# A written order on TensorE for the routing rounds of a two-layer mixture of experts: 27 steps of three held-back products in each round

## The chip, the core and the metric

The kernel runs on one core of a Trainium2 chip. The metric is the time of one execution on the device in microseconds, as the median of several runs. Five engines work in parallel, each through its own queue of instructions in order: TensorE (PE) multiplies matrices into PSUM banks, VectorE (DVE) and ScalarE (ACT) work elementwise, GpSimd (POOL) does elementwise work, reductions over partitions and indirect DMAs, and SyncE (SP) issues most of the other DMAs. The loading of a matrix into PE ahead of a product is listed apart, as PEld.

## What is computed

Sparse attention, then two mixtures of experts on its output. In the first every token goes through all eight experts, weighted by a Sinkhorn-normalised table; in the second every token gets one expert, taken greedily in the order of the logits, with room for 192 tokens per expert.

```python
x = attention(q, k, v)              # 2 x 8 heads x 768 x 64 -> 1536 tokens x 512
# first layer: N=1536, D=512, E=8 experts, F=1024
P = sinkhorn(exp(x @ w_gate))       # 8 rounds
for e in range(E):
    out += P[:, e:e+1] * (np.maximum(x @ w1[e], 0.0) @ w2[e])
# second layer, on out
logits = x @ w_gate
for idx in np.argsort(-logits.flatten()):
    tok, e = idx // E, idx % E
    if assigned[tok] >= 0 or counts[e] >= cap:   # cap = N // E = 192
        continue
    assigned[tok] = e; counts[e] += 1
for e in range(E):
    mask = assigned == e
    out[mask] = np.maximum(x[mask] @ w1[e], 0.0) @ w2[e]
```

## The kernel before

*Tiles.* Tokens are worked on in 12 blocks of 128 (`NC`), in three token blocks of 512 (`NTB`). Every fp32 operand is split into two fp16 parts, so each contraction over 128 takes three products: high by high, high by low, low by high (`mm3`, lines 664 to 666). A hidden block (`ph`) of one expert and one token block goes into a `hslot`; from it come four accumulations (`py`), one per 128 tokens, of 8 x 3 = 24 products of 512 columns each. The result goes, weighted, into the sum `acc`.

*Held-back work.* The first layer's second products of expert 7 and expert 6 are not done when their hidden blocks are ready. The list `post` holds them: (6,2), (7,0), (7,1), (7,2), (6,0), (6,1), as (expert, token block), in all 6 x 4 x 24 = 576 products. The hidden blocks of (6,0) and (6,1) wait in DRAM and come back (`get_back`) into the slots of the first two entries of `post`, when these are used up. The results of all but the last entry are evicted by ACT (line 760, into one of three `relu` buffers) and added by POOL (line 761); those of the last are added by DVE (line 765). ACT then takes the largest absolute value of each finished block of `acc` (`absj`, line 686). Calls of `expert_out` for `post` are written behind the whole routing.

*Gate.* The logits `L` of the second layer depend linearly on what each expert adds, so the share of expert 7 is worked out ahead of its held-back products: twelve small products `pg` (lines 138 and 139 hold their last two parts), one per 128 tokens, each read from its PSUM bank by two DVE instructions (lines 144 and 145) before the next may use that bank.

*Routing.* Seven rounds (line 918). Each has a `propose` on DVE (each token's best free expert, its weight `w`, the 0/1 table `B8`); 12 transposes `pw` on PE (line 925), which lay the weights out along the free axis, copied out by ACT and DVE (`raw`); comparisons of every weight with every other, by DVE (lines 953, 955, 956) and for token blocks 0, 4 and 8 by ACT (lines 946 to 950), into `xt`; three groups of 12 count products `pr` (line 961), each behind four token blocks of comparisons; copies of the counts (`spill`, lines 971 and 973); 12 products `prc` (line 976); two DVE instructions (lines 978 and 983; X in `rBT`, sum `rT`), for which POOL has prepared `rBT` (lines 932 to 934); one sum over partitions `prs` on PE (line 985); and six DVE instructions that update `L`. Behind the seventh come a last `propose`, 12 products `pk` (lines 999 and 1001), and the slots `si`.

*Behind the routing.* POOL scatters the rows of `acc` to their slots in DRAM (`xg`, line 1034, twelve indirect DMAs), and reduces the largest absolute value `xam` over the partitions (line 102), from which the scale of the second layer follows. Rows of two experts are read back, transposed by PE (`px`, line 1087), scaled by ACT (line 1089), and the second layer begins with `ph`. Its weights, split and put away in DRAM before, come by SP's queue into slots that become free, those of the held-back hidden blocks among them.

*What sets the order.* A scheduler places the instructions of each engine: written order gives the priority, and an instruction whose inputs come late lets later ones go ahead. The held-back products are written last, so they fill what it takes to be gaps: 49 between the twelve gate products, 369 in the first six rounds (61 to 63 in each), 53 in the seventh up to its `prs`, 13 from there to `pk`, and 92 behind `pk`.

Of the kernel before, what the change touches and what calls it, by code (L numbers as in the profile page):

```python
# [20 lines left out]
P = 128  # L21
# [19 lines left out]
def tile_sparse_attention_moe_moe(ctx, tc, q, k, v, ng, nl, wg1, w11, w12, wg2, w21, w22, out, taps=None):  # L41
# [10 lines left out]
    TB = 512  # L52
# [697 lines left out]
    def expert_out(e, tb, by_pool=False):  # L750
# [3 lines left out]
        for t in range(CPB):  # L754
# [3 lines left out]
            if by_pool:  # L758
                y = rawp.tile([P, TB], F32, name="relu", bufs=3)
                nc.scalar.activation(y[:, :DM], ps, AF.Copy, scale=pf[:, c:c + 1])  # L760
                nc.gpsimd.tensor_tensor(acc[:, c, :DM], acc[:, c, :DM], y[:, :DM], op=ALU.add)  # L761
            elif e == 0:
                nc.vector.tensor_scalar(acc[:, c, :DM], ps, pf[:, c:c + 1], None, op0=ALU.mult)
            else:
                nc.vector.scalar_tensor_tensor(acc[:, c, :DM], ps, pf[:, c:c + 1], acc[:, c, :DM],
                                               op0=ALU.mult, op1=ALU.add)

# [147 lines left out]

    NQ = NT // 512
    on_act = (0, 4, 8)
    for rnd in range(E - 1):
        w = propose()
        wr = rawp.tile([P, NT], F32, name="raw", bufs=2)  # L920
        for n in range(NQ):
            pt = aux([P, 4, P], name="pw")
            for c in range(4):
                cc = 4 * n + c
                nc.tensor.transpose(pt[:, c, :], w[:, cc:cc + 1].to_broadcast([P, P]), ident)
            if n == 1:
# [10 lines left out]
        for c in range(NC):  # L937
# [20 lines left out]
            if c % 4 == 3:  # L958
                def count(n, cc):
                    j = 32 * (cc % 4)  # L960
                    return nc.tensor.matmul(pr[n][j:j + 32, :], Bp[:, cc, :], gs[cc][:, n * 512:n * 512 + 512],
                                            start=cc < 4, stop=cc >= NC - 4, tile_position=(0, j))
# [12 lines left out]
        for c in range(NC):  # L975
            nc.tensor.matmul(pc[:, c, :], rs[:, c * P:c * P + P], comb, start=True, stop=True)
# [8 lines left out]
        nc.tensor.matmul(T.rearrange("p a e -> p (a e)"), ones, R.rearrange("p a e -> p (a e)"), start=True, stop=True)  # L985
# [9 lines left out]
    propose()  # L995

    pk = misc([P, NC, E], name="pk")
    for n in range(1, NC):
        nc.tensor.matmul(pk[:, n if n > 1 else 0:, :], onesb, Bz[:, 1 if n > 1 else 0:NC + 1 - n, 0:E],
                         start=n == 1, stop=False)  # L1000
    nc.tensor.matmul(pk, before, B8, start=False, stop=True)
# [11 lines left out]
    for n, (e, tb) in enumerate(post):  # L1013
# [165 lines left out]
```

## Time and profile before

| | us |
|---|---|
| median of 3 runs | 1388.05 (1387.29 to 1388.94) |
| the profiled execution, its own time | 1384.17 |
| its span, from first to last instruction | 1382.3 |
| PE busy | 1308.7 |
| DVE busy | 808.3 |
| ACT busy | 591.8 |
| POOL busy | 211.3 |

Times in the rows below count from the start of the span. Idle time in brackets stands ahead of an instruction, with what ended it. The granted clock is TensorE's: 1.00 is 2.4 GHz, 0.50 is 1.2 GHz; over the whole execution it was 0.987 in the mean. A PE row's length is modelled at its end, so consecutive products overlap; how fast they follow one another is read from the starts.

### The profile page before, as it was taken

How to read it: one execution, taken by the hardware profiler on the slowest of the kernel's cores; microseconds unless marked ns; L12 is line 12 of the kernel's file. 1: busy time of each engine (PE TensorE's matmuls, PEld its weight loads, DVE VectorE, ACT ScalarE, POOL GpSimd, SP SyncE). 2: the span in 40 equal slices, each digit the busy share in tenths (PEclk: the TensorE clock that was granted, in tenths of full speed). 3: DMA queues.
4: the chain of work that ended last, by engine and by line, in shares of the span. 5: the costliest groups of instructions: out<-in, count | busy, mean ns of one | idle time of the engine just before them, and what ended most of it. 6: DMA issues, size and time to landing. Idle time of an engine off the chain costs nothing.

```text
span 1382.3 us, 19944 instructions
## 1 busy us (share of the span) xinstructions
PE 1308.7 (95%) x7956; PEld 670.7 (49%) x7956; DVE 808.3 (58%) x1765; ACT 591.8 (43%) x1053; POOL 211.3 (15%) x323
## 2 busy tenths in 40 slices
PE   5899999999999999999899999999999989879998
PEld 3665544444444444444344444445545434337775
DVE  5777686554666466556546655575635898822121
ACT  3667551343243324333522434166553566613332
POOL 5233211010001000000100010000001333430100
PEclk8999999999999999999999999999999999989999
DMA  8352024151545135324424441431001111378640
GB/s 217 82 150 74 1 74 170 61 197 47 173 145 170 61 126 179 122 87 158 149 95 142 143 160 57 169 123 62 2 1 63 62 62 62 122 208 302 273 201 24
DMA packets 88557, 164.93 MB, mean 119 GB/s; under 512 B 50065, under 2 KB 50065, under 8 KB 85905
## 3 DMA queue, kind: packets, MB, share of 16 engines
q1 hardware_dynamic: 77040, 119.62, 26.7%
q0 software_dynamic: 11424, 44.05, 8.3%
q8 instruction: 62, 1.02, 0.3%
q14 instruction: 31, 0.25, 0.1%
HBM read 119.61 MB, written 44.05 MB: 118 GB/s over the span
## 4 chain that ended last, share of the span: by engine, by line
PE 47%; DVE 15%; issue 15%; DMA 13%; ACT 5%; POOL 5%; POOLq 0%; DVEq 0%; ACTq 0%
DMA raw<-in_moe_w_dram 7%; PE ph L664 7%; PE ph L666 7%; PE ph L665 7%; PE py L664 6%; PE py L665 6%; PE py L666 6%; DMA ws<-spill 6%; DVE wam L607 4%; DVE wslot L619 2%; POOL acc L761 2%; PE pe L491 2%; PE pa L510 2%; DVE xt L953 1%; DVE xt L955 1%
## 5 line engine op out<-in xcount | busy, mean ns | idle before, releaser
L664 PE MATMUL py<-wslot,hslot 128*128 128x512 f16 x768 | 291.3, 379 | 9.9 <-ACT relu L658 9.9
L664 PE MATMUL ph<-xt,wslot 128*128 128x512 f16 x768 | 291.4, 379 | 7.4 <-ACT relu L658 3.9
L665 PE MATMUL py<-wslot,hslot 128*128 128x512 f16 x768 | 291.3, 379 | 0.0
L666 PE MATMUL py<-wslot,hslot 128*128 128x512 f16 x768 | 291.3, 379 | 0.0
L666 PE MATMUL ph<-xt,wslot 128*128 128x512 f16 x768 | 291.3, 379 | 0.0
L665 PE MATMUL ph<-xt,wslot 128*128 128x512 f16 x768 | 291.2, 379 | 0.0
L657 ACT ACTIVATE hslot<-ph 128x512 f16<-128x512 f32 x192 | 114.5, 596 | 208.9 <-PE ph L666 208.7
L659 DVE TENSOR_TENSOR hslot<-relu,hslot 128x512 f16<-128x512 f32 x192 | 131.5, 688 | 119.6 <-ACT relu L658 118.6
L607 DVE TENSOR_REDUCE wam<-raw 128x1 f32<-128x1024 f32 (+1 forms) x136 | 152.5, 1149 | 74.6 <-DMA raw<-in_moe_w_dram 74.5
L618 ACT ACTIVATE spill<-raw,s 128x1024 f16<-128x1024 f32 x64 | 72.8, 1146 | 246.4 <-DVE s L114 129.8
L619 DVE SCALAR_TENSOR_TENSOR spill<-raw,s,spill 128x1024 f16<-128x1024 f32 x64 | 81.7, 1284 | 114.4 <-ACT spill L618 113.2
L658 ACT ACTIVATE relu<-ph 128x512 f32<-128x512 f32 (+1 forms) x224 | 130.1, 581 | 0.0
L665 PEld LDWEIGHTS <-hslot 128*128 128x128 f16 x768 | 75.3, 98 | 98.9 <-issue 13.6
L665 PEld LDWEIGHTS <-wslot 128*128 128x128 f16 x768 | 75.1, 98 | 93.8 <-issue 9.5
L664 PEld LDWEIGHTS <-hslot 128*128 128x128 f16 x768 | 75.3, 98 | 88.6 <-issue 2.5
L666 PEld LDWEIGHTS <-hslot 128*128 128x128 f16 x768 | 75.1, 98 | 88.5 <-issue 2.5
L666 PEld LDWEIGHTS <-wslot 128*128 128x128 f16 x768 | 75.1, 98 | 87.4
L664 PEld LDWEIGHTS <-wslot 128*128 128x128 f16 x768 | 75.1, 98 | 87.4 <-issue 2.4
L618 ACT ACTIVATE wslot<-raw,s 128x1024 f16<-128x1024 f32 (+1 forms) x72 | 70.9, 1047 | 72.3 <-PE py L666 48.7
L619 DVE SCALAR_TENSOR_TENSOR wslot<-raw,s,wslot 128x1024 f16<-128x1024 f32 (+1 forms) x72 | 81.2, 1159 | 4.3 <-ACT wslot L618 4.3
L650 POOL DMA_DIRECT2D ws<-spill x64 | 44.2, 692 | 220.8 <-DVE spill L619 220.5
L102 POOL PARTITION_ALL_REDUCE amax<-wam x30 | 10.6, 354 | 413.9 <-DVE wam L608 406.0
(245 smaller groups left out, 1652.6 us busy)
## 6 DMA issues: line engine op xcount, KB each, us to landing
raw<-in_moe_w_dram SPq DMA_DIRECT2D x64, 1024.0 KB, 5.9
ws<-spill POOLq DMA_DIRECT2D x64, 512.0 KB, 6.6
w2slot<-ws SPq DMA_DIRECT2D x16, 2048.0 KB, 10.2
hd<-hslot POOLq DMA_DIRECT2D x2, 2048.0 KB, 7.2
hslot<-hd SPq DMA_DIRECT2D x2, 2048.0 KB
qb<-in_q_dram SPq DMA_DIRECT2D x12, 256.0 KB, 3.4
kb<-in_k_dram SPq DMA_DIRECT2D x12, 256.0 KB, 6.6
vo<-in_v_dram SPq DMA_DIRECT2D x12, 256.0 KB, 3.7
```

What stands on the lines that cost most here:

```text
L491: nc.tensor.transpose(pe[:ck, y, j, :], ex[:, y, j, a * P:a * P + ck], ident)
L510: nc.tensor.matmul(S.pa[64 * j:64 * j + 64, p, :], S.vs[a][:ck, 2 * p + j, :], ets[a][:ck, y, j, :], start=a == 0, stop=a == S.nch - 1, ti ...
L607: nc.vector.tensor_reduce(am[:, y:y + 1], raw, axis=AX.X, op=ALU.max, apply_absolute_value=True)
L618: nc.scalar.activation(hi, raw, AF.Copy, scale=s[:, 0:1])
L619: nc.vector.scalar_tensor_tensor(lo, raw, s[:, 0:1], hi, op0=ALU.mult, op1=ALU.subtract)
L650: nc.gpsimd.dma_start(dr[:, :, a * q4:a * q4 + q4], t)
L657: nc.scalar.activation(hi, ps, AF.Relu, scale=HS)
L658: nc.scalar.activation(r[:, :n], ps, AF.Relu, scale=HS)
L659: nc.vector.tensor_sub(lo, r[:, :n], hi)
L664: nc.tensor.matmul(out_, lhs(0, a), rhs(0, a), start=a == 0, stop=False)
L665: nc.tensor.matmul(out_, lhs(0, a), rhs(1, a), start=False, stop=False)
L666: nc.tensor.matmul(out_, lhs(1, a), rhs(0, a), start=False, stop=a == n - 1)
```

## The change

The held-back products get a place in the program. `expert_out` for `post` is gone; a generator `held_back` issues the same products, and yields after each step of three. `run(n)` issues the next n steps, and stands in the round at six places: seven steps behind the transposes `pw`, four, eight and two behind the three groups of counts, three behind `prc`, three behind `prs`. So a round has 27 steps, 81 products. Two more steps are behind the last `propose`, ahead of `pk`; what is left of the 192 steps, one, is issued behind the slots.

`pin` is a new mark on PE's instructions (`tc.keep_in_program_order`): those that bear it keep the order in which they are written. All products of the rounds, `pk` and the held-back products bear it. The counts no longer bear the rule that set a group behind its first product (`issue_after`). `get_back` is written ahead of the rounds. How the held-back results are evicted and added stays as it was.

```diff
+    pin = tc.keep_in_program_order
+
+    def held_back(e, tb, by_pool):
...
+        for t in range(CPB):
+            c = tb * CPB + t
+            ps = mmbank([P, DM], name="py")
+            for f in range(FC):
+                for n, (y1, y2) in enumerate(((0, 0), (0, 1), (1, 0))):
+                    pin(nc.tensor.matmul(ps, h[:, y1, f, t * P:t * P + P], w[:, y2, f, :],
+                                         start=f == 0 and n == 0, stop=f == FC - 1 and n == 2))
+                if f == FC - 1:
...
+                yield
...
+    for n, (e, tb) in enumerate(post):
+        if (e, tb) in away:
+            m = n - len(post) + len(away)
+            get_back(e, tb, NTB * post[m][0] + post[m][1])
+
+    def all_held():
+        for e, tb in post:
+            yield from held_back(e, tb, (e, tb) != post[-1])
+
+    held = all_held()
+
+    def run(n):
+
+        for _ in range(n):
+            next(held, None)
+
     NQ = NT // 512
     on_act = (0, 4, 8)
     for rnd in range(E - 1):
...
-                nc.tensor.transpose(pt[:, c, :], w[:, cc:cc + 1].to_broadcast([P, P]), ident)
+                pin(nc.tensor.transpose(pt[:, c, :], w[:, cc:cc + 1].to_broadcast([P, P]), ident))
...
+        run(7)
...
-                first = count(0, c)
-                with tc.issue_after(first.ins):
-                    for n in range(NQ):
-                        for cc in range(c - (n == 0), c - 4, -1):
-                            count(n, cc)
+                    pin(nc.tensor.matmul(pr[n][j:j + 32, :], Bp[:, cc, :], gs[cc][:, n * 512:n * 512 + 512],
+                                         start=cc < 4, stop=cc >= NC - 4, tile_position=(0, j)))
+                for n in range(NQ):
+                    for cc in range(c, c - 4, -1):
+                        count(n, cc)
+                run((4, 8, 2)[c // 4])
...
-            nc.tensor.matmul(pc[:, c, :], rs[:, c * P:c * P + P], comb, start=True, stop=True)
+            pin(nc.tensor.matmul(pc[:, c, :], rs[:, c * P:c * P + P], comb, start=True, stop=True))
+        run(3)
...
+        pin(nc.tensor.matmul(T.rearrange("p a e -> p (a e)"), ones, R.rearrange("p a e -> p (a e)"), start=True,
+                             stop=True))
+        run(3)
...
     propose()
+    run(2)
...
+    finish(held)
...
-    for e, tb in post:
-        expert_out(e, tb, (e, tb) != post[-1])
```

The first place is on PE, between the last gate product and the first round's transposes. Before, with held-back products (`py`) there:

```order
L139 MATMUL pg<-vg7hl,hslot 128x16
L666 LDWEIGHTS hslot
L666 MATMUL py<-wslot,hslot 128x512
L664 LDWEIGHTS hslot
L664 MATMUL py<-wslot,hslot 128x512
L665 LDWEIGHTS hslot
L665 MATMUL py<-wslot,hslot 128x512
L666 LDWEIGHTS hslot
L666 MATMUL py<-wslot,hslot 128x512
L664 LDWEIGHTS hslot
L664 MATMUL py<-wslot,hslot 128x512
L925 MATMUL pw<-ident,rw 128x128 x12
```

and now, where the transposes follow at once:

```order
L138 LDWEIGHTS hslot
L138 MATMUL pg<-vg7hl,hslot 128x16
L139 LDWEIGHTS hslot
L139 MATMUL pg<-vg7hl,hslot 128x16
L961 MATMUL pw<-ident,rw 128x128 x12
```

All 49 products that stood between and behind the gate products have moved into the rounds.

The second place is on ACT, in the sixth round, from the last comparisons (into `xt`) to the next round's copies (`raw`). Before:

```order
L946 ACTIVATE xt<-raw,rw 128x1024
L949 ACTIVATE xt<-raw,rw 128x384
L947 ACTIVATE xt<-xt 128x1024
L950 ACTIVATE xt<-xt,ones 128x384
L760 ACTIVATE relu<-py,pf 128x512
L686 ACTIVATE absj,xam<-acc 128x512 x2
L973 ACTIVATE spill<-pr 128x512 x2
L760 ACTIVATE relu<-py,pf 128x512
L686 ACTIVATE absj,xam<-acc 128x512
L929 ACTIVATE raw<-pw 128x512 x2
```

Now:

```order
L986 ACTIVATE xt<-raw,rw 128x384
L686 ACTIVATE absj,xam<-acc 128x512
L987 ACTIVATE xt<-xt,ones 128x384
L686 ACTIVATE absj,xam<-acc 128x512
L781 ACTIVATE relu<-py,pf 128x512
L686 ACTIVATE absj,xam<-acc 128x512
L1009 ACTIVATE spill<-pr 128x512 x2
L781 ACTIVATE relu<-py,pf 128x512
L686 ACTIVATE absj,xam<-acc 128x512
L965 ACTIVATE raw<-pw 128x512 x2
```

Ahead of the two copies of the counts stand three `absj` with one eviction now, where two `absj` and one eviction stood.

The third place is on POOL, from the last round's `rBT` to the scatters of the output at the kernel's end. The two ISA rows are the load of the reduction's code and the reduction over the partitions. Before:

```order
L934 TENSOR_TENSOR rBT<-rBT,tok 128x96
L761 TENSOR_TENSOR acc<-acc,relu 128x512 x3
L1034 DMA xg<-acc,si 1536x513 x12
L102 ISA
L102 ISA amax<-xam 128x1
L1042 DMA out_dram<-spill,idx 1536x512 x12
```

Now:

```order
L971 TENSOR_TENSOR rBT<-rBT,tok 128x96
L1069 DMA xg<-acc,si 1536x513
L102 ISA
L102 ISA amax<-xam 128x1
L1069 DMA xg<-acc,si 1536x513 x11
L1077 DMA out_dram<-spill,idx 1536x512 x12
```

No add of a held-back result is left behind the seventh round's `rBT`, and the load and the reduction stand behind the first scatter, no longer behind the twelfth. SP's queue has the same order as before.

## Rows read from the trace of the kernel before

**Rows 1.** The head of the profile page: the span of the profiled execution, and the busy time, share of the span and instructions of each engine.

```profile
span 1382.3 us, 19944 instructions
...
PE 1308.7 (95%) x7956; PEld 670.7 (49%) x7956; DVE 808.3 (58%) x1765; ACT 591.8 (43%) x1053; POOL 211.3 (15%) x323
```

**Rows 2.** Busy time by stretch, from the span's start: the stretch and its length; PE busy (instructions), PEld, DVE, ACT, POOL likewise; the granted TensorE clock (1.00 is full speed); the DMA share; GB/s. In order of time these are the gate products after the last hidden product up to the first round's `pw`; the first `pw` to the seventh round's `prs`; within it the second round alone, `pw` to `pw`; the end of the seventh round and the 92 held-back products behind it; and from there to the first product of the second layer.

```profile
1047.35:1062.95 15.60, 15.58 (x242) 9.43 (x241) 9.18 (x39) 1.79 (x4) 1.27 (x1) 1.00 0.38 138
...
1062.95:1208.55 145.60, 128.48 (x855) 58.09 (x855) 127.46 (x301) 93.79 (x130) 56.50 (x39) 1.00 0.19 73
...
1084.01:1104.29 20.28, 18.55 (x124) 8.40 (x124) 18.10 (x45) 12.89 (x17) 9.31 (x5) 1.00 0.14 58
...
1208.55:1232.25 23.70, 23.57 (x119) 10.68 (x119) 5.83 (x19) 3.58 (x9) 11.89 (x12) 1.00 0.76 211
...
1232.25:1242.80 10.55, 2.42 (x10) 1.68 (x10) 1.60 (x8) 1.36 (x4) 1.33 (x2) 0.60 0.50 162
```

**Rows 3.** Timeline of PE in the second round: start and length in us, engine, line, operation, output <- inputs, shapes, count, and in brackets the idle time before it and what ended it.

```profile
1084.01 1.52 PE L925 MATMUL pw<-ident,rw 128*128 128x128 f32 x12
...
1085.37 0.38 PE L666 MATMUL py<-wslot,hslot 128*128 128x512 f16 x1
...
1089.47 0.38 PE L664 MATMUL py<-wslot,hslot 128*128 128x512 f16 x1
...
1097.17 0.38 PE L665 MATMUL py<-wslot,hslot 128*128 128x512 f16 x1
...
1098.74 0.83 PE L961 MATMUL pr<-xt,Bz 128*32 128x512 bf16 x12 [1.19 <-DVE xt L953]
...
1100.41 0.34 PE L976 MATMUL prc<-comb,spill 128*128 128x8 f16 x8
...
1102.18 0.37 PE L985 MATMUL prs<-rT,ones 128*128 128x24 f32 x2 [0.33 <-DVE rT L983]
...
1104.29 1.52 PE L925 MATMUL pw<-ident,rw 128*128 128x128 f32 x12
```

**Rows 4.** Waits from the first `pw` to the seventh `prs`: who waited for whom, us in all, times, the longest.

```profile
ACT absj L686 <- POOL acc L761: 10.1, 7, 2.3
...
PE pr L961 <- DVE xt L953: 7.8, 7, 1.2
...
PE prc L976 <- ACT spill L973: 2.8, 3, 1.3
```

**Rows 5.** Timeline of POOL, DVE, PE and ACT: the add of a held-back product in a pause of DVE (first row), and then the sixth round.

```profile
1080.94 1.09 POOL L761 TENSOR_TENSOR acc<-acc,relu 128x512 f32<-128x512 f32 x1 [3.74 <-ACT relu L760]
...
1175.10 7.99 POOL L761 TENSOR_TENSOR acc<-acc,relu 128x512 f32<-128x512 f32 x2 [5.44 <-ACT relu L760]
...
1178.25 0.34 DVE L955 TENSOR_SCALAR xt<-raw,rw 128x256 bf16<-128x256 f32 x1
...
1179.57 1.18 DVE L955 TENSOR_SCALAR xt<-raw,rw 128x128 bf16<-128x128 f32 x1
...
1181.93 0.83 PE L961 MATMUL pr<-xt,Bz 128*32 128x512 bf16 x12 [1.02 <-DVE xt L953]
...
1183.12 0.63 ACT L686 ACTIVATE absj<-acc 128x512 bf16<-128x512 f32 x1 [1.70 <-POOL acc L761]
...
1183.75 1.06 ACT L973 ACTIVATE spill<-pr 128x512 f16<-128x512 f32 x2
```

**Rows 6.** Timeline of PE and DVE for one of the twelve gate products: its first and last product on PE, and DVE's two instructions that read the PSUM bank.

```profile
1058.94 0.17 PE L138 MATMUL pg<-vg7hl,hslot 128*128 128x16 f16 x1
...
1059.32 0.17 PE L139 MATMUL pg<-vg7hl,hslot 128*128 128x16 f16 x1
...
1059.53 0.23 DVE L144 SCALAR_TENSOR_TENSOR gt<-pg,vfc,L 128x8 f32<-128x8 f32 x1 [0.58 <-PE pg L139]
...
1059.79 0.23 DVE L145 SCALAR_TENSOR_TENSOR L<-pg,vfc,gt 128x8 f32<-128x8 f32 x1
```

**Rows 7.** Busy time by stretch in the attention part, columns as in rows 2.

```profile
46.00:49.00 3.00, 1.05 (x4) 0.67 (x4) 2.98 (x9) 1.10 (x4) 0.10 (x1) 1.00 1.05 238
...
50.00:56.00 6.00, 5.55 (x24) 4.13 (x22) 4.85 (x19) 3.07 (x10) 2.42 (x6) 0.50 0.02 4
```

**Rows 8.** Timeline of PE, POOL and DVE from the last round's `prs` to the first product of the second layer.

```profile
1208.55 0.37 PE L985 MATMUL prs<-rT,ones 128*128 128x24 f32 x2 [0.32 <-DVE rT L983]
...
1211.82 0.47 PE L999 MATMUL pk<-Bz,onesb 128*128 128x96 bf16 x11
...
1213.95 1.20 POOL L1034 DMA_INDIRECT xg<-acc,si  x1 [1.19 <-DVE si L1009]
...
1215.45 0.96 POOL L1034 DMA_INDIRECT xg<-acc,si  x1 [0.30 <-issue]
...
1232.25 0.75 DVE L765 SCALAR_TENSOR_TENSOR acc<-py,pf,acc 128x512 f32<-128x512 f32 x1 [4.43 <-PE py L666]
...
1233.28 0.95 POOL L1034 DMA_INDIRECT xg<-acc,si  x1 [4.22 <-DVE acc L765]
...
1239.45 0.90 PE L1087 MATMUL px<-ident,raw 128*128 128x128 f32 x3 [7.24 <-DMA raw<-xg]
...
1240.30 0.38 POOL L102 PARTITION_ALL_REDUCE amax<-xam  x1 [6.07 <-issue]
...
1242.80 0.80 PE L664 MATMUL ph<-xt,w2slot 128*128 128x192 f16 x4 [0.46 <-ACT xt L1089]
```

More of the change, by code (lines that the diff above doesn't have):

```diff
@@ L748, in factors, with expert_out @@
         pfs[e] = pf
-    def expert_out(e, tb, by_pool=False):
+    def expert_out(e, tb):
         h = hs.pop((e, tb))
@@ L757, in expert_out @@
             mm3(ps, lambda z, f: h[:, z, f, t * P:t * P + P], lambda z, f: w[:, z, f, :], FC)
[L758 to L762, printed above, removed]
+            if e == 0:
                 nc.vector.tensor_scalar(acc[:, c, :DM], ps, pf[:, c:c + 1], None, op0=ALU.mult)
@@ L766, in expert_out @@
                                                op0=ALU.mult, op1=ALU.add)
+    pin = tc.keep_in_program_order
+    def held_back(e, tb, by_pool):
+        h = hs.pop((e, tb))
+        w, _ = W[e, 1]
+        pf = pfs[e]
+        for t in range(CPB):
[6 more added lines that the diff above has]
+                if f == FC - 1:
+                    if by_pool:
+                        y = rawp.tile([P, TB], F32, name="relu", bufs=3)
+                        nc.scalar.activation(y[:, :DM], ps, AF.Copy, scale=pf[:, c:c + 1])
+                        nc.gpsimd.tensor_tensor(acc[:, c, :DM], acc[:, c, :DM], y[:, :DM], op=ALU.add)
+                    else:
+                        nc.vector.scalar_tensor_tensor(acc[:, c, :DM], ps, pf[:, c:c + 1], acc[:, c, :DM],
+                                                       op0=ALU.mult, op1=ALU.add)
+                yield
     waiting = []
@@ L984, in tile_sparse_attention_moe_moe @@
         T = misc([P, 3, E], name="prs")
-        nc.tensor.matmul(T.rearrange("p a e -> p (a e)"), ones, R.rearrange("p a e -> p (a e)"), start=True, stop=True)
+        pin(nc.tensor.matmul(T.rearrange("p a e -> p (a e)"), ones, R.rearrange("p a e -> p (a e)"), start=True,
+                             stop=True))
+        run(3)
         tau = rsm.tile([P, E], F32, name="rtau")
@@ L995, in tile_sparse_attention_moe_moe @@
     propose()
+    run(2)
     pk = misc([P, NC, E], name="pk")
     for n in range(1, NC):
-        nc.tensor.matmul(pk[:, n if n > 1 else 0:, :], onesb, Bz[:, 1 if n > 1 else 0:NC + 1 - n, 0:E],
-                         start=n == 1, stop=False)
-    nc.tensor.matmul(pk, before, B8, start=False, stop=True)
+        pin(nc.tensor.matmul(pk[:, n if n > 1 else 0:, :], onesb, Bz[:, 1 if n > 1 else 0:NC + 1 - n, 0:E],
+                             start=n == 1, stop=False))
+    pin(nc.tensor.matmul(pk, before, B8, start=False, stop=True))
     sl = rsm.tile([P, NC, E], F32, name="sl")
@@ L1009, in tile_sparse_attention_moe_moe @@
     nc.vector.tensor_copy(si, sf)
+    finish(held)
     if "slot" in taps:
         nc.sync.dma_start(taps["slot"].rearrange("(c p) -> p c", p=P), si)
-    for n, (e, tb) in enumerate(post):
-        if (e, tb) in away:
-            m = n - len(post) + len(away)
-            get_back(e, tb, NTB * post[m][0] + post[m][1])
-    for e, tb in post:
-        expert_out(e, tb, (e, tb) != post[-1])
     if "x2" in taps:
```

2 lines of the change are left out of this document (removed).

## The prediction

> **What bounds the kernel now.** I read the head of the page first: TensorE (PE) is busy for 1308.7 of 1382.3 us, so that over the whole span there is little idle time that any order could fill [rows 1]. The change touches only the stretch from the last hidden product to the second layer, so the second view is busy time by stretch, there alone [rows 2]. The reader is to see three stretches with different limits. In the gate stage PE is full: 15.58 of 15.60 us. From the first `pw` to the seventh `prs` it is busy for 128.48 of 145.60 us and idle for 17.1. Then it is full again for 23.7 us, and after that it does next to nothing for 10.6 us.
>
> The third view, PE's timeline in one round, shows who sets a round's pace: the third count group waits 1.19 us for VectorE's compares, and `prs` 0.33 us for a VectorE sum [rows 3]. VectorE is busy for 18.10 of the round's 20.28 us, but PE for 18.55 [rows 2]: it is the second limit, only 1.7 us below. The fourth view, the waits over the rounds, says the same in sum, and shows ScalarE (ACT) waiting 10.1 us for GpSimd's (POOL's) adds and `prc` 2.8 us behind that [rows 4].
>
> **The change, step by step.** The counts of products are counted from the two program orders. From the first `pw` to the seventh `prs` there were 422 (369 in six rounds, 53 in the seventh); now there are 558 (6 x 81 + 72). The 49 between the gate products become none, and behind the seventh `prs` 13 and 92 become 15 and 3. No product is added or saved.
>
> *Rounds.* One held-back product takes 0.216 us: 19 of them from 1085.37 to 1089.47 [rows 3]. 136 more are 29.3 us. The idle 17.1 us can take that much and no more, so the rounds grow by 12.2 us at the least. For one round: 18.55 + 20 x 0.216 = 22.9 us of PE work where the round took 20.28. That is more than VectorE's 18.10, ACT's 12.89 and POOL's 9.31 [rows 2], so PE becomes the bound: between the second and third count groups ten more products (2.2 us) stand where 1.19 us were idle, nine instead of five hold up `prs`, nine instead of eight `pw`.
>
> *Waits that stay in the rounds.* PE's order is now fixed, so a wait ahead of `prc` stops the products behind it too. In the sixth round ACT's new order has three `absj`, each waiting for a POOL add, ahead of the two `spill` copies that `prc` needs. Beside VectorE's compares two adds took 7.99 us where one alone takes 1.09; the second was done, and `absj` began, 1.2 us after the third count group had started (1183.12 against 1181.93) [rows 5]. That group now starts 1.1 us later after `pw`, the add does not; so at about its start ACT still has `absj` 0.7, an eviction 0.7, an add 1.1, `absj` 0.7 ahead of the copies' 1.06: some 4.5 us with the gaps, where PE gets to `prc` after 0.8 + 6 x 0.216 + 0.1 = 2.2. That is 2.3 us. An add also holds VectorE: the 128-wide compare took 1.18 us beside one, a 256-wide one without it 0.34 [rows 5]. In the first, second, fourth and fifth rounds an accumulation now closes after the third count group, and its add falls on VectorE's short chain to `pw`: four times 0.85, about half of it covered by PE's own products, is 1.8. Together 4.1 us. The ends are 0 (all of it covered) and 9 (the longest wait of `prc`, 1.3 [rows 4], in each of seven rounds); a gain is excluded, since the floor is PE's own work. I take 4.1, near the row of the sixth round.
>
> *Gate stage.* Without products between them the twelve gate products run at their own latency: 0.38 us from the first to the last matmul's start, 0.21 until VectorE reads the bank, 0.49 for its two instructions [rows 6], and some 0.05 (an estimate with no row of its own) until PE starts again: 1.13 each. 11 x 1.13 + 1.08 + 0.4 for the first maximum is 13.9 us instead of 15.6: a gain of 1.7. The 10.6 us of products that were there cost 10.6 in the rounds; that is the poor trade.
>
> *Clock.* In that stage PE is now busy for about 0.55 of each 1.13 us. The nearest row is in the attention part: 1.05 us of work in 3 was followed by six us at a granted clock of 0.50, which is 1.2 GHz, though PE was busy again for 5.55 of them [rows 7]. So I expect the first round to begin at half speed for five to six us, which costs 2.5. The ends are 0 and 3.5. The Trainium skill, "TensorE: Matmul & The Clock Gate", Part 1, says that the throttled clock is the default and that activity releases it. By that rule sparse work loses the clock, and the 2.5 stand; without it the sum below would be 16.7.
>
> *Tail.* 92 products (19.8 us) covered something: POOL's scatters. The first needs the slots, the rest follow at 0.96 + 0.30 = 1.26 us each [rows 8], eleven in all behind the first. After the last came the load of the partition reduction's code: 6.07 us without an instruction ahead of a reduction of 0.38 [rows 8]. POOL's new order has one scatter, this load, the reduction, and then eleven scatters. From the last `prs`: `pk` at 3.65 (15 products instead of 13; before 3.27), the first scatter 2.13 later as before [rows 8], plus 0.75 for the last accumulation, which VectorE now does in between, at 6.5. Then 1.20 + 6.07 + 0.38 + 0.30 + 10 x 1.26 = 20.6: the last scatter starts at 27.1, where it started at 24.7 (1233.28 - 1208.55). That is 2.4 us later. The scale is ready earlier now, but the transposes of the gathered rows waited for the scatter in any case; the first product came 3.35 us after the first transpose [rows 8], and I take 0.3 of that back (ends 0 and 1.5). Sum: 2.1 us later, between 0.5 and 2.5. So the products leave the tail, and nothing of it gets shorter: PE stands idle there for some 28 us instead of ten. The Trainium skill, "GPSIMD Engine Reference", 2.1 Instruction dispatch, says that the first call into a freshly loaded kernel pays about 6 us that no instruction shows, measured 5.95. It speaks against this change, and the trace agrees with 6.07; by the page's figure the sum would be 0.1 lower.
>
> *At no cost.* The two reloads of hidden activations are written ahead of the rounds, but wait for the same products (the 96th and 192nd, now in the second and third rounds) and are needed only for the 385th, in the fifth; if that cover were gone, PE would wait for their landing. SP's queue has the same order as before. The code for POOL's elementwise adds is now loaded within the first round, between two steps of `rBT`; these are needed only behind the compares, over ten us later.
>
> **The sum** is -1.7 + 12.2 + 4.1 + 2.5 + 2.1 = +19.2 us. The profiled execution took 1384.17 us (span 1382.3), which gives 1403.4; the median of the three runs, 1388.05, is 3.9 above it, which gives 1407.
>
> **Rivals.** *The clock holds.* The gate products may keep the clock up; the row that I took is from another part of the kernel, where PE did less before the clock fell. Then 2.5 us less: 1405. *The adds cost more.* The rounds now have 20 POOL adds where they had 18, each late one can hold both VectorE and ACT, and PE can no longer fill such a hole; with twice the 4.1 and one us in the seventh round, whose four evictions are now VectorE's, it is 1412. *The load is not in the way.* If POOL's code load ran while the slots are awaited, the tail would be 6 us shorter: 1401. Against it: the load comes in POOL's order behind the first scatter, which itself waits for the slots. *Faster: the rounds keep VectorE's pace.* If a round's work other than held-back products, which I count as 18.55 - 61 x 0.216 = 5.4 us, were mostly overlap of modelled ends, 81 products could fit into 20.28 us; that needs at most 2.8 us for `pw`, three count groups, `prc` and `prs`. All rounds at 20.28, with the seventh to its `prs` at 18.2, make 139.9 instead of 145.6, no clock or wait is felt, and the kernel is at -5.7 - 1.7 + 2.1 = -5.3: 1383. Against it: `pw` alone holds PE for 1.36 us before the next product starts, and the third count group starts 1.67 us before the last `prc` [rows 3]. From 3.7 us per round on it would be no faster.
>
> **How the numbers follow.** Forecast 0.50, and its own range 1403 to 1411; clock holds 0.20; adds cost more 0.14; load not in the way 0.08; rounds at VectorE's pace 0.04; 0.04 for what I don't see. The forecast is the likeliest, 1407. The low end, 1397, takes in the short tail together with a clock that holds; the high end, 1413, the adds. About 0.2% (2.8 us) is what a measurement of this kernel can tell from no change. All cases but the last two are slower by more than that: slower 0.93, the same 0.03, faster 0.04.
>
> **What would show it.** Right: a round of about 22.9 us from `pw` to `pw` with PE without idle time; no wait of `pr` for VectorE; a granted clock near 0.5 at the start of the first round; a longer sixth round with `prc` waiting for `spill`; on POOL one scatter, six empty us, the reduction and eleven scatters, and PE idle from `pk` to `px` for over 25 us. Wrong: rounds that stay near 20.5 us; scatters that end within 20 us of the last `prs`; a clock of 1.00 throughout.

## The result and the profile after

The changed kernel takes 1403.76 us, median of four runs (1401.56 to 1406.19), beside 1387.67 for the kernel before. The ratio is 1.0135, 95% interval 1.0115 to 1.0156: it is slower, by some 16 to 22 us. The forecast was 1407, 19 us slower, with 1403 to 1411 as its own range: the time lies inside it, near the low end. The two profiled executions, from which the stages below are read, are 22.0 us apart (1406.19 and 1384.17).

The head of the changed kernel's page, which answers to [rows 1]:

```profile
span 1404.4 us, 19931 instructions
...
PE 1312.8 (93%) x7956; PEld 674.2 (48%) x7956; DVE 808.7 (58%) x1765; ACT 592.1 (42%) x1053; POOL 208.0 (15%) x323
```

PE has the same 7956 products and 4 us more of busy time. Its share falls from 95 to 93% because the span is longer. So most of the loss, some 18 of the 22 us, is idle time of PE, and the head doesn't say where. The table of busy time by stretch does. It answers to [rows 2], with the same columns: the gate stage; the first `pw` to the seventh `prs`; the first to the sixth round alone; the seventh up to its `prs`; and from there to the second layer.

```profile
1049.26:1063.76 14.50, 7.03 (x194) 5.93 (x192) 8.21 (x39) 1.08 (x2) 0.00 (x0) 0.60 0.39 148
1063.76:1226.00 162.24, 155.73 (x990) 71.78 (x991) 130.42 (x304) 97.46 (x138) 54.59 (x41) 0.98 0.21 79
1063.76:1089.99 26.23, 24.92 (x143) 11.68 (x144) 18.95 (x45) 13.28 (x17) 4.83 (x6) 0.89 0.00 1
1089.99:1112.24 22.25, 22.08 (x143) 10.19 (x144) 18.00 (x45) 13.16 (x17) 11.86 (x6) 1.00 0.26 95
1112.24:1135.30 23.06, 22.09 (x144) 10.15 (x144) 18.80 (x45) 13.54 (x18) 6.90 (x6) 1.00 0.25 92
1135.30:1158.87 23.57, 22.25 (x144) 10.10 (x144) 19.32 (x45) 14.08 (x20) 10.99 (x7) 1.00 0.25 90
1158.87:1181.12 22.25, 22.08 (x144) 10.21 (x145) 18.16 (x45) 14.89 (x23) 10.36 (x6) 1.00 0.18 61
1181.12:1204.54 23.42, 22.23 (x144) 10.20 (x144) 19.14 (x45) 15.57 (x24) 7.90 (x7) 1.00 0.33 130
1204.54:1226.00 21.46, 20.08 (x133) 9.26 (x133) 18.06 (x40) 12.94 (x20) 1.74 (x4) 1.00 0.23 92
1226.00:1264.46 38.46, 6.97 (x42) 3.80 (x41) 5.24 (x25) 2.08 (x6) 12.40 (x13) 0.59 0.39 118
```

Against [rows 2]: the gate stage is 1.1 us shorter (14.50, was 15.60) and now only half full. The rounds are 16.6 us longer (162.24, was 145.60), with PE busy for 155.73 of them. The stretch behind the last `prs` is 4.2 us longer (38.46, was 23.70 + 10.55 = 34.25), and PE is idle for over 31 of its 38 us. Together that is +19.8. The last hidden product ended 1.9 us later than before, with an order that is the same up to there, and the second layer took 0.4 more; with these it is the 22.1 us between the two spans (1404.4 and 1382.3).

Three kinds of round can be told apart. The second and fifth, 22.25 us, are PE's own work: 22.08 of it. The third, fourth and sixth are 0.8 to 1.3 longer with the same work on PE; the seventh, which is counted only up to its `prs`, has 1.4 us of waits. The first is four us longer, at a granted clock of 0.89 in the mean. The clock us by us, same columns, in the gate stage and in the first round:

```profile
1050.76:1051.76 1.00, 0.23 (x10) 0.13 (x7) 0.93 (x4) 0.00 (x0) 0.00 (x0) 1.00 0.58 180
1051.76:1052.76 1.00, 0.51 (x16) 0.41 (x16) 0.82 (x5) 0.00 (x0) 0.00 (x0) 0.73 0.80 344
1052.76:1053.76 1.00, 0.59 (x16) 0.50 (x16) 0.43 (x4) 0.00 (x0) 0.00 (x0) 0.50 0.99 426
...
1067.76:1068.76 1.00, 1.00 (x4) 0.34 (x3) 1.00 (x4) 1.00 (x2) 0.00 (x0) 0.50 0.00 0
1068.76:1069.76 1.00, 1.00 (x5) 0.35 (x4) 1.00 (x3) 1.00 (x2) 0.00 (x0) 0.74 0.00 0
1069.76:1070.76 1.00, 1.00 (x6) 0.49 (x5) 1.00 (x3) 1.00 (x2) 0.00 (x0) 1.00 0.00 0
```

The clock fell to 0.50 (1.2 GHz) some three us after the hidden products ended, and came back 5.5 us after the first `pw` at 1063.76. That is 17 us at half speed, of which the first round has five and a half.

One wait in the sixth round, from the timelines of POOL, DVE and PE:

```profile
1185.38 1.27 POOL L782 TENSOR_TENSOR acc<-acc,relu 128x512 f32<-128x512 f32 x1 [2.02 <-ACT relu L781]
...
1185.41 1.38 DVE L993 SCALAR_TENSOR_TENSOR xt<-raw,rw,tie 128x128 bf16<-128x128 f32 x1
...
1188.10 0.83 PE L998 MATMUL pr<-xt,Bz 128*32 128x512 bf16 x12 [0.98 <-DVE xt L993]
```

A comparison on VectorE (DVE) that takes 0.34 us elsewhere in the round took 1.38 beside POOL's add, and the first counts waited 0.98 us. And the end of the routing, timelines of POOL and PE, which answer to [rows 8]:

```profile
1232.03 1.20 POOL L1069 DMA_INDIRECT xg<-acc,si  x1 [24.55 <-DVE si L1049]
1240.44 0.38 POOL L102 PARTITION_ALL_REDUCE amax<-xam  x1 [7.21 <-issue]
1241.02 1.20 POOL L1069 DMA_INDIRECT xg<-acc,si  x1 [0.20 <-issue]
...
1253.92 0.96 POOL L1069 DMA_INDIRECT xg<-acc,si  x1 [0.30 <-issue]
...
1261.17 0.90 PE L1122 MATMUL px<-ident,raw 128*128 128x128 f32 x3 [30.62 <-DMA raw<-xg]
```

One scatter, 7.21 us without an instruction, the reduction, eleven scatters; the last starts 27.9 us after the last `prs` (1226.00), where it was 24.7.

### The profile page after: what moved, and what is told of

It is laid out like the page before. It is cut to its first block, busy times and chain, and to the rows that moved or that the text cites. A ratio compares the mean times of both kernels' runs of the same rounds, so it can differ in the third digit from the quotient of the medians.

```text
span 1404.4 us, 19931 instructions
## 1 busy us (share of the span) xinstructions
PE 1312.8 (93%) x7956; PEld 674.2 (48%) x7956; DVE 808.7 (58%) x1765; ACT 592.1 (42%) x1053; POOL 208.0 (15%) x323
## 5 line engine op out<-in xcount | busy, mean ns | idle before, releaser
L664 PE MATMUL py<-wslot,hslot 128*128 128x512 f16 x576 | 219.7, 381 | 10.5 <-ACT relu L658 10.5
L666 PE MATMUL py<-wslot,hslot 128*128 128x512 f16 x576 | 219.6, 381 | 0.0
L665 PE MATMUL py<-wslot,hslot 128*128 128x512 f16 x576 | 219.6, 381 | 0.0
L776 PE MATMUL py<-wslot,hslot 128*128 128x512 f16 x576 | 132.8, 382 | 0.0
```

The lines of the kernel that those rows point to most:

```text
L664: nc.tensor.matmul(out_, lhs(0, a), rhs(0, a), start=a == 0, stop=False)
L665: nc.tensor.matmul(out_, lhs(0, a), rhs(1, a), start=False, stop=False)
L666: nc.tensor.matmul(out_, lhs(1, a), rhs(0, a), start=False, stop=a == n - 1)
L776: pin(nc.tensor.matmul(ps, h[:, y1, f, t * P:t * P + P], w[:, y2, f, :], start=f == 0 and n == 0, stop=f == FC - 1 and n == 2))
```

## The experiments

Every ratio is to the kernel before, over the runs of its own session. The kernel before took 1387.67 us in the session of the change, 1384.16 in that of the next four kernels (up to 24 steps), 1386.12 in that of the three behind them and 1384.61 in that of the last three, so medians of different sessions are compared by their ratios.

| kernel | median us | ratio | 95% interval |
|---|---|---|---|
| the change | 1403.76 | 1.0135 | 1.0115 to 1.0156 |
| cover in the gate stage | 1400.74 | 1.0113 | 1.0088 to 1.0139 |
| load behind the scatters | 1396.15 | 1.0083 | 1.0062 to 1.0104 |
| without POOL's adds | 1396.83 | 1.0090 | 1.0066 to 1.0114 |
| 24 steps | 1385.06 | 1.0004 | 0.9992 to 1.0016 |
| 24 steps, other places | 1387.10 | 1.0015 | 0.9998 to 1.0033 |
| 13 steps in the gate stage | 1390.18 | 1.0028 | 1.0010 to 1.0046 |
| 13 in the gate stage, 22 a round | 1381.53 | 0.9965 | 0.9948 to 0.9982 |
| the same, `absj` behind the rounds | 1376.01 | 0.9943 | 0.9926 to 0.9960 |
| the same, 23 in four rounds | 1375.64 | 0.9939 | 0.9918 to 0.9960 |
| before, `absj` behind the rounds | 1379.48 | 0.9967 | 0.9950 to 0.9985 |

These are the lengths of the stages in the profiled executions, one of each kernel, in us: from the last hidden product to the first `pw`, the six rounds, the seventh to its `prs`, and from there to the last scatter's start and to the second layer's first product.

| kernel | gate | 1 | 2 | 3 | 4 | 5 | 6 | 7 | scatter | layer 2 |
|---|---|---|---|---|---|---|---|---|---|---|
| before | 15.6 | 21.06 | 20.28 | 21.05 | 20.27 | 21.75 | 21.76 | 19.43 | 24.7 | 34.3 |
| the change | 14.5 | 26.23 | 22.25 | 23.06 | 23.57 | 22.25 | 23.42 | 21.46 | 27.9 | 38.5 |
| cover | 15.3 | 22.95 | 22.25 | 23.05 | 23.56 | 22.25 | 23.43 | 21.46 | 27.5 | 38.2 |
| load behind | 14.5 | 26.20 | 22.25 | 23.06 | 23.56 | 22.25 | 23.43 | 21.47 | 20.2 | 31.3 |
| without adds | 14.5 | 23.45 | 22.19 | 22.19 | 22.20 | 22.20 | 22.19 | 20.77 | 27.9 | 40.1 |
| 24 steps | 14.5 | 23.67 | 21.64 | 21.82 | 21.99 | 21.83 | 22.19 | 20.28 | 20.0 | 30.9 |
| 24, other places | 14.4 | 23.72 | 20.71 | 20.86 | 21.05 | 22.46 | 22.83 | 20.66 | 22.6 | 32.2 |
| 13 in the gate | 14.8 | 22.11 | 23.97 | 22.25 | 23.59 | 23.29 | 22.25 | 20.00 | 19.7 | 30.3 |
| 13, 22 a round | 14.8 | 20.88 | 20.19 | 20.49 | 21.01 | 21.89 | 22.10 | 19.38 | 22.4 | 31.7 |
| `absj` behind | 14.8 | 20.88 | 20.18 | 20.48 | 21.02 | 20.95 | 20.01 | 18.50 | 22.3 | 32.2 |
| 23 in four | 14.8 | 20.22 | 20.99 | 20.01 | 20.88 | 20.84 | 21.00 | 17.81 | 19.8 | 31.1 |
| before, `absj` | 15.6 | 21.06 | 20.26 | 21.06 | 20.28 | 20.80 | 20.90 | 18.17 | 25.2 | 34.5 |

**Cover in the gate stage.** The edit, behind each gate product of expert 7:

```diff
+            if e == E - 1:
+                w2 = W[E - 2, 1][0]
+                ps = mmbank([P, DM], name="py")
+                for k in range(4):
+                    nc.tensor.matmul(ps, hs[E - 2, NTB - 1][:, 0, k, 0:P], w2[:, 0, k, :], start=k == 0, stop=k == 3)
```

> The changed kernel with four products of its own after each of the twelve gate products (48, work added, whose results are not used), so that PE is busy there again. Theory (the clock): the first round took 26.2 us where the undisturbed second took 22.25, because the granted clock fell to 0.50 in the emptied gate stage; with the cover the clock stays at 1.00, the first round takes 22.3 us (-4.0), the gate stage some 15.6 (+1.1): 2.9 us faster than the changed kernel, about 1401. Rival (the load of POOL's code within the first round, or the fixed order, makes the first round long): the clock is back at 1.00 and the first round still takes 25 us or more; the kernel is about 1 us slower than the changed one, 1405.

Busy time of the gate stage and of the first round, columns as before:

```profile
1046.34:1061.67 15.33, 15.33 (x241) 9.34 (x239) 8.21 (x39) 1.08 (x2) 0.00 (x0) 1.00 0.39 140
...
1061.67:1084.62 22.95, 22.23 (x145) 10.13 (x144) 17.94 (x45) 13.16 (x17) 9.82 (x6) 1.00 0.00 1
```

and, from the timelines of POOL and PE, the end of that round:

```profile
1082.71 1.09 POOL L782 TENSOR_TENSOR acc<-acc,relu 128x512 f32<-128x512 f32 x1 [4.43 <-ACT relu L781]
...
1084.62 1.52 PE L966 MATMUL pw<-ident,rw 128*128 128x128 f32 x12 [0.63 <-DVE rw L932]
```

The clock stays at 1.00, the first round is 3.3 us shorter, and no other round moves by more than 0.01. In the ratios of whole runs the intervals of this kernel and of the change overlap; the stages settle it. The clock costs 3.3 us here. Of these, 2.7 are PE's longer work (24.92 us busy against 22.23), and the other 0.6 are waits: in the change the second counts of this round waited 0.68 us for a comparison beside an add, and with the cover they don't. The 0.7 us by which this round is longer than the second are another matter: 0.63 of them are `pw` waiting for VectorE, with an add of POOL beside that short chain. The rival falls.

**Load behind the scatters.** The two lines that make the scale are moved:

```diff
-    nc.vector.tensor_reduce(xam[:, NC:], xam[:, :NC], axis=AX.X, op=ALU.max)
-    sx2 = pow2_scale(xam[:, NC:], "sx2")
...
         scs.append(st)
+    nc.vector.tensor_reduce(xam[:, NC:], xam[:, :NC], axis=AX.X, op=ALU.max)
+    sx2 = pow2_scale(xam[:, NC:], "sx2")
```

> The changed kernel with the reduction of the largest value, and the load of its code, written behind the twelve scatters; POOL's order is then as it was before the change. Theory (the load stands in the way of eleven scatters): the last scatter starts 20.0 us after the last prs instead of 27.9, the first transpose of the gathered rows at 27.2 instead of 35.2, the scale comes at 28.2, and the second layer begins 30 us after that prs instead of 38.5: 8 us faster than the changed kernel, about 1396. Rival (the landing of the scatters or of the weights sets the second layer's start): the scatters start early, but the first transpose moves by less than 2 us; 1402 to 1404.

POOL's timeline, the first and the last scatter and the reduction:

```profile
1230.91 1.20 POOL L1067 DMA_INDIRECT xg<-acc,si  x1 [24.55 <-DVE si L1049]
...
1245.06 0.96 POOL L1067 DMA_INDIRECT xg<-acc,si  x1 [0.30 <-issue]
1252.72 0.38 POOL L102 PARTITION_ALL_REDUCE amax<-xam  x1 [6.70 <-issue]
```

The last scatter starts 20.2 us after the last `prs` (1224.89), and the second layer 31.3 after that `prs`: 7.2 less, with every round as it was. The load takes 6.70 us here too, but beside the landing of the scatters. The theory holds, with 7.2 of its 8 us. That the median is 1396.15 where 1396 was expected is in part the session, in which the kernel before is 3.5 us faster.

**Without POOL's adds.** The line `nc.gpsimd.tensor_tensor(acc..., acc..., y...)` in `held_back` is left out, so that the sum lacks these results.

> The changed kernel without POOL's 20 additions of the held-back results (work left out; the sum lacks them). Theory (an addition on POOL holds VectorE's short comparisons, and PE waits for these in the third, fourth, sixth and seventh rounds): these rounds, 0.8 to 1.3 us above the 22.25 of the second and fifth, come down to it; 4.6 us less: about 1399. Rival (VectorE is late there by itself, or by ACT's comparisons): the waits stay, within 1 us of the changed kernel.

DVE's groups by form over the rounds: lines of the changed kernel, the comparison within a token block and the narrowest one beside it (count, busy us, mean ns):

```profile
L993 DVE SCALAR_TENSOR_TENSOR xt<-raw,rw,tie 128x128 bf16<-128x128 f32 x84 | 29.7, 366 | 0.0
L992 DVE TENSOR_SCALAR xt<-raw,rw 128x128 bf16<-128x128 f32 x7 | 6.8, 975 | 0.0
```

and the same two without the adds:

```profile
L992 DVE SCALAR_TENSOR_TENSOR xt<-raw,rw,tie 128x128 bf16<-128x128 f32 x84 | 27.6, 341 | 0.0
...
L991 DVE TENSOR_SCALAR xt<-raw,rw 128x128 bf16<-128x128 f32 x7 | 2.1, 300 | 0.0
```

Busy time by stretch of the first and the second round without the adds:

```profile
1062.89:1086.34 23.45, 23.45 (x144) 11.49 (x145) 17.24 (x45) 13.16 (x17) 6.56 (x3) 0.93 0.00 1
1086.34:1108.53 22.19, 22.02 (x145) 10.14 (x144) 17.01 (x45) 13.16 (x17) 0.97 (x3) 1.00 0.26 96
```

Rounds two to six are 22.19 or 22.20 us, of which PE is busy for 22.02 or 22.03; a wait of 0.17 us is left in each. So what the change's rounds two to seven have above these lengths, 4.3 us in sum, comes from POOL's adds. The first round has no idle time on PE either, and is 2.8 us shorter than in the change, also because the clock came back earlier. The second layer's start is 1.7 us later here, behind the same last scatter: 0.9 us of it stand ahead of the first transpose of the gathered rows and 0.8 in a wait among the transposes, both for rows that are read back. Why they come later is open.

The Trainium skill, "SBUF — State Buffer", Who interferes with whom, says that a VectorE instruction with two SBUF inputs contends with a GpSimd instruction that reads SBUF, and that the pair of ports which the two share is an exclusive lock. The 1.38 us of the sixth round, 0.34 plus most of an add, agrees with that. Over all rounds the narrowest comparison of line 992, which reads one tensor, loses more (4.7 us) than those of line 993, which read two (2.1).

**24 steps a round.** `run((4, 8, 2)[c // 4])` becomes `run((4, 5, 2)[c // 4])`.

> The changed kernel with 24 steps a round instead of 27: five instead of eight behind the second group of counts. 22 steps, 66 products, are left for behind the last prs, and POOL's order at the end has the load behind the scatters again. Theory (PE bounds the rounds): each round is shorter by 9 x 0.216 = 1.94 us, to 20.3 where the second round now takes 22.25; in all 13.5 us less from the first pw to the last prs, and 8 us less behind it, where the 66 products lie beside the scatters: about 1382. Rival (the rounds are long because of waits that the fixed order brings): the rounds stay above 21.5 us, -5 there, -8 behind: about 1391.

PE's timeline in the second round:

```profile
1090.90 0.83 PE L998 MATMUL pr<-xt,Bz 128*32 128x512 bf16 x12 [0.68 <-DVE xt L993]
...
1099.47 0.83 PE L998 MATMUL pr<-xt,Bz 128*32 128x512 bf16 x12 [0.58 <-DVE xt L990]
1100.23 1.47 PE L776 MATMUL py<-wslot,hslot 128*128 128x512 f16 x6
1101.54 0.44 PE L1012 MATMUL prc<-comb,spill 128*128 128x8 f16 x12
1101.84 2.10 PE L776 MATMUL py<-wslot,hslot 128*128 128x512 f16 x9
1103.78 0.30 PE L1022 MATMUL prs<-rT,ones 128*128 128x24 f32 x2
```

Of the 21.5 us that were expected the stages give 16.4, and the theory is half wrong. PE has 20.2 us of work in a round, as worked out, but the round is 21.64, above the 21.5 of the rival: PE waits for VectorE (0.17 + 0.68 + 0.58 us). Three steps less gave 0.6 us in this round, not 1.94. At 27 steps PE is the bound; at 24, with these places, PE waits for VectorE's comparisons; whether POOL's adds have a part in that, no run shows. The crossing is at about 26 steps, by an estimate (22.25 less 0.65 for each step meets 21.64). The stretch behind the last `prs` gave 7.5: POOL's order is again twelve scatters and then the load, and the 66 products beside them cost nothing.

**24 steps at other places.** The six numbers become 8, 4, 6, 1, 2, 3.

> Again 24 steps a round, as in the kernel with 24 steps before it (7, 4, 5, 2, 3, 3 at the six places), but at other places: 8, 4, 6, 1, 2, 3. One step less stands between the third counts and prc, and one less between prc and prs, where in that kernel's second round prc started 0.45 us after ACT's copies were done and prs 0.5 us after VectorE's sum; one more stands behind pw and one behind the second counts, where PE waited 0.68 and 0.58 us for VectorE. Theory (at 24 steps a round is VectorE's chain, lengthened by products that stand in it): about 0.9 us less in each round, 20.75 where it was 21.64; 6 us in all, 1379. Rival (the number of products sets the round, or VectorE's comparisons beside POOL's additions do): the rounds stay within 0.3 us, 1385.

Rounds two to four are 0.9 us shorter, as the theory has it: where products stand counts as much as how many there are. But the fifth and sixth are 0.6 longer, and the sum is no gain: the rounds are 1.1 us shorter in all, where 6 were expected, and the stretch behind them is 1.3 longer. PE's `prc` in the fifth round:

```profile
1165.14 0.74 PE L1012 MATMUL prc<-comb,spill 128*128 128x8 f16 x12 [1.12 <-ACT spill L1009]
```

ACT's timeline ahead of it:

```profile
1163.88 0.63 ACT L686 ACTIVATE absj<-acc 128x512 bf16<-128x512 f32 x1 [1.38 <-POOL acc L782]
...
1164.51 1.06 ACT L1009 ACTIVATE spill<-pr 128x512 f16<-128x512 f32 x2
```

With one step less ahead of `prc`, an `absj` that waits for a POOL add holds up `prc`. This is the wait that the prediction had put into the changed kernel.

**Steps in the gate stage.** `held` is defined earlier, and the gate stage takes 13 steps:

```diff
     for tb in range(NTB):
-        late_logits(E - 1, tb)
+        late_logits(E - 1, tb, lambda: run(1))
+    run(1)
```

Once with 27 steps a round:

> The changed kernel with 13 of its own steps between and behind the gate products, 27 a round as before, so that the held-back work ends within the seventh round and nothing is left behind it. POOL then has the load and the reduction ahead of all twelve scatters. Theory: gate stage 15.3 (+0.8), first round 22.9 (-3.3), seventh round 19.5 to its prs (-2), and the load runs while the slots are awaited, so the last scatter starts 20 us after the last prs (-8, as far as the second layer's start -7): 1392. Rival (a load ahead of the scatters costs its 7 us there also, because it starts only with the slots): 1399.

POOL's reduction and first scatter:

```profile
1218.89 0.38 POOL L102 PARTITION_ALL_REDUCE amax<-xam  x1 [15.60 <-DVE xam L1066]
1226.59 1.20 POOL L1072 DMA_INDIRECT xg<-acc,si  x1 [7.33 <-DVE si L1052]
```

The reduction stands 2.2 us ahead of the last `prs` (1221.05), so the load lies in time in which POOL had nothing else to do, and cost nothing: the last scatter started 19.7 us after that `prs`. By the stages it is 12.6 us below the change, where 12 were expected, though the second and fifth rounds are 1.7 and 1.0 us longer. Then with 22 steps a round, at 7, 4, 5, 1, 2, 3:

> A written order with the products where the earlier runs found room: one step after each of the twelve gate products and one more behind them, 22 steps a round at 7, 4, 5, 1, 2, 3, two ahead of pk, and 23 (69 products) behind it, beside the scatters. Theory: gate stage 15.3 us, no fall of the clock, first round near the others at 20.5 (was 23.67 with 24 steps and an empty gate stage); last scatter 20 us after the last prs, second layer at 31: 8 us less than the kernel with 24 steps at the first places, about 1377, and 0.5% below the kernel before the change. Rival (the chain of VectorE takes 21 us with its additions however the products stand, as the 21.6 to 22.2 with 24 steps): rounds 21.3, about 1382, no clear gain over the kernel before.

This one is faster than the kernel before by 0.35%, less than the 0.5% of the theory; the time is the rival's, and so is the mean of the six rounds, 21.1 us. The first four are near 20.5 us, as the theory has it, the fifth and sixth 21.9 and 22.1. In the sixth `prc` stands behind `absj` and `spill` once more:

```profile
1185.09 0.74 PE L1015 MATMUL prc<-comb,spill 128*128 128x8 f16 x12 [1.62 <-ACT spill L1012]
```

In the seventh it waits 0.77 us. In the fifth it doesn't wait; there the first counts wait 0.95 us for a comparison beside an add.

**`absj` behind the rounds.** `with tc.issue_after(copied.ins):` is put around the twelve `absj`, `copied` being ACT's last copy of the counts.

> The written order of the run before it (13 steps in the gate stage, 22 a round at 7, 4, 5, 1, 2, 3), with ACT's twelve absj put behind the last round's copies of the counts. Theory (in the fifth and sixth rounds, 21.9 and 22.1 us, an absj that waits for a POOL addition stands ahead of the copies that prc needs): both rounds come down to 20.4, 3 us less, about 1378.5; the tail has room for the twelve, 9 us of ACT. Rival (POOL's additions, which hold VectorE, make these rounds long): they stay above 21.5, 1381.5.

The fifth and sixth rounds, busy time by stretch:

```profile
1144.44:1165.39 20.95, 19.44 (x130) 8.74 (x129) 18.92 (x45) 13.07 (x17) 13.22 (x6) 1.00 0.14 58
1165.39:1185.40 20.01, 19.16 (x129) 8.77 (x129) 17.98 (x45) 12.89 (x17) 10.59 (x5) 1.00 0.54 210
```

They are 0.9 and 2.1 us shorter, the seventh 0.9, and the four before them the same. No `prc` waits for `spill` in any round now. That is the theory's gain in the sixth and seventh. The fifth had no such wait, and its 0.9 us have another cause. One add of POOL there, and two comparisons on VectorE, in the kernel of the run before:

```profile
1150.29 1.89 POOL L782 TENSOR_TENSOR acc<-acc,relu 128x512 f32<-128x512 f32 x1 [2.62 <-ACT relu L781]
...
1150.97 1.61 DVE L996 SCALAR_TENSOR_TENSOR xt<-raw,rw,tie 128x128 bf16<-128x128 f32 x2
```

and here:

```profile
1149.32 8.55 POOL L782 TENSOR_TENSOR acc<-acc,relu 128x512 f32<-128x512 f32 x1 [2.63 <-ACT relu L781]
...
1149.99 0.60 DVE L996 SCALAR_TENSOR_TENSOR xt<-raw,rw,tie 128x128 bf16<-128x128 f32 x2
```

The order is the same, and the add starts within 0.02 us of the same place. Once the add got through and the comparisons were held, once the comparisons ran and the add took 8.55 us. So single rounds can differ by 0.9 us by which of the two came first.

The kernel is 0.57% faster than the one before the change. The interval overlaps with that of the run before it (0.9926 to 0.9960 and 0.9948 to 0.9982); the sixth and seventh rounds are what shows the gain.

With 23 steps in the first four rounds:

> The same, with one step more behind the second counts of the first four rounds, where PE waited 0.8 us for VectorE; 12 products less stand behind pk. Theory: the four rounds stay within 0.1 us, and the last scatter, which waited for the last sum until 22.4 us after the last prs, comes at 20: 2 us less than its neighbour, about 1376.5. Rival (VectorE has no room left, or the last scatter waits for something else): within 0.5 us of its neighbour.

The four rounds don't stay as they were: the first and third are 0.7 and 0.5 us shorter, the second 0.8 longer, in sum 0.5 less. The last scatter comes 2.5 us earlier, but the second layer only 1.1, and the median gives 0.4 us: the rival's figure. This is the fastest version here, but not to be told from its neighbour. And the same edit of `absj` alone, in the kernel before:

> The kernel before the change with only ACT's twelve absj put behind the last round's copies. Theory (its fifth and sixth rounds, 21.75 us each against 20.3 for the second and fourth, have the same cause): 3 us less than the kernel before, 0.2%. Rival: the scheduler's order or POOL's additions make them long; no change.

0.33% faster: the fifth, sixth and seventh rounds are 20.80, 20.90 and 18.17 us instead of 21.75, 21.76 and 19.43, together 3.1 us. The 2.8 us that `prc` waited for `spill` [rows 4] are gone, which shows the cause. So the place of ACT's `absj` alone gives 0.33%, the written order alone 0.35%, and both together 0.57%; the intervals don't tell which of the two is worth more. Beside `absj` the written order still counts: in the same session the medians with and without it are 1376.01 and 1379.48.

## Why the prediction was right, and by how much each step was

The sign and the time were right, and so were the five parts, each with its sign. Measured in the stages above:

| term | forecast us | measured us |
|---|---|---|
| gate stage | -1.7 | -1.1 |
| rounds, PE's own work | +12.2 | +8.3 |
| waits in the rounds | +4.1 | +5.0 |
| clock | +2.5 | +3.3 |
| tail | +2.1 | +4.2 |
| sum | +19.2 | +19.7 |

That the sums are within 0.5 us is luck: the rounds were 3.9 us too large, and the other four terms together 4.4 too small. The medians of the runs, 16 us apart, put the change lower than the stages of the two profiled executions do.

*Rounds.* The mechanism was right: PE became the bound. Without adds, six rounds at 22.19 and a seventh at 20.77 are 153.9 us, 8.3 more than the 145.60 before. The size was too large by 3.9. The step that failed is "The idle 17.1 us can take that much and no more". A round of 22.19 us holds 81 products at 0.216, which leaves 4.7 us for its other work, where I had read 5.4 out of [rows 2]: a row of a single product is 0.38 long, though the next could start after 0.216, and where a product stood ahead of a wait its modelled end was counted as busy. By the starts of its rows, PE's waits in the second round before the change come to some 2.7 us; the busy column leaves 1.73. The rival with rounds at VectorE's pace had named this; it was true for 0.7 us a round, not for the 2.6 that it needed.

*Waits.* The sum was near, 4.3 in rounds two to seven, where the run without POOL's adds shows the cause, and 0.7 in the first. That is luck too, for the places were mostly wrong. The 2.3 us put at `prc` in the sixth round were at most 0.2: the add ahead ended earlier, after 4.24 us, and the two steps ahead of `prc` covered the rest. That this wait is real was seen only where a step less stood there. The adds on VectorE's chain to `pw`, put into four rounds, held `pw` in the first and the fourth (0.64 and 0.52 us), not in the second and fifth. What there was instead is a wait of the first counts, 0.63 to 0.98 us in the third, fourth, sixth and seventh rounds, for a comparison held by an add, where "no wait of `pr` for VectorE" was to be seen. One reading was wrong, too: the comparison of 256 called free of the add lies within the 7.99 us of the two adds [rows 5], so an add doesn't hold each comparison that it meets. The rival with twice the waits was not borne out.

*Clock.* It fell, as forecast, and the first round began with 5.5 us at half speed; 3.3 lies within the ends given, 0 and 3.5. It is the figure of one execution: without the adds, where the clock came back after 3.2 us, the first round is 1.3 us above the others. The rival in which it holds was wrong. *Gate stage.* Each product took some 1.18 us at the lower clock instead of 1.13.

*Tail.* The order on POOL did what was said. The load took 7.21 us instead of 6.07, and from the last scatter's start to the first transpose it took 7.25 instead of 6.17. These two make 2.2 us of the 2.1 that were missing; the rest nearly cancels, a first scatter 0.5 us earlier than forecast against small items. The run with the load behind the scatters gives back 7.2. The rival in which the load is not in the way was wrong here, and true of the kernel whose held-back work ended within the seventh round.

*At no cost.* That held: PE waited for no reload, and the 7.45 us on POOL between two steps of `rBT` in the first round held up nothing.

What stays open: why the load takes 6.1 us in one execution and 7.3 in another (7.21 in the change and 6.85 with the cover, where POOL's order is the same), and the few us by which equal code ahead of the gate stage differs between executions (the last hidden product ended from 1046.0 to 1051.8).

## What to carry to other kernels

Work that fills the waits of an engine was free here only up to the pace of the engine that it waits for, and only at the places where it waits: 24 steps at one set of places took 21.64 us in the second round, at another 20.71. Ahead of moving filler, look at what it covered where it stood (a clock, a queue of scatters, a load), and price that in the stage where it stood. And look at who holds the short chain before the bound engine's order is written out: one edit of ScalarE's order gave the old kernel 0.33%, about as much as the whole written order alone.

## What was not expected

- The clock fell with PE idle for only 0.58 to 0.77 us at a time (0.23 to 0.51 busy in each us up to the fall). It came back 5.5 us after the first `pw` in the change and 3.2 in the run without adds, with the same order on PE; in the five kernels with an empty gate stage it took from 3.2 to 5.9. With products between the gate products, four or three for each, it stayed at 1.00.
- A last scatter that follows the one before it after 0.30 us took 7.3 to 8.2 us to the first transpose; one that came after 2.8 us or more of idle time on POOL took 5.9 to 6.3. So an earlier last scatter gave back only part (2.5 us earlier, 1.1 gained).
- The same load of POOL's code showed as 6.06 to 7.26 us in the eleven kernels in which nothing covers it. The Trainium skill, "GPSIMD Engine Reference", 2.1 Instruction dispatch, has it at about 6; the rows here are up to 1.3 above that.
- An add and a comparison that met held one another: an add that takes 1.09 us alone took up to 7.21 in the change, and in the same order now the one lost time and now the other.
